# Moving first loads, one broadcast and a load schedule at the opening of a kernel's second pass

## The chip, the cores and the metric

The kernel runs on one core of a Trainium2 chip. The metric is the device time of one execution in microseconds (us); the number compared is the median of several runs. One further execution is recorded by the hardware profiler, and all line numbers and times inside the kernel come from that one.

## What is computed

The layer mixes two branches of the same input `x` (2048 rows of 576), and the kernel returns the output and the gradients of seven tensors (`B_x` is a constant and is not used):

```python
g = sigmoid((x * gate_w).sum(-1))              # one gate per row
a = irfft2(rfft2(x) * (w_r + 1j * w_i))        # branch A: a spectral filter
b = (gelu(x @ w_gate) * (x @ w_up)) @ w_down   # branch B: hidden width 4608
out = g * a + (1 - g) * b
# returned: out, and the gradients of x, w_r, w_i, w_gate, w_up, w_down, gate_w for grad_out
```

## The kernel before

**Two passes.** Pass one goes over the hidden width in 18 groups. It computes the hidden activations and their gradients, writes both to DRAM scratch (`scr`), forms the gradients of the three weight matrices, and beside this work runs the forward transforms of branch A and of its gradient. It leaves the spectra in DRAM scratch (`scr_p1` for the output, `scr_p2` for the gradient of `x`). Pass two, from about 919 us on, goes over the 16 row tiles of 128 rows. It multiplies the scratch by `w_down` (job "b", the output of branch B), by the transposed `w_gate` (job "g") and by the transposed `w_up` (job "u"); "g" and "u" of a tile add into one pair of accumulators and give the gradient of `x`. The last tile has both in one job "x". The list `jobs` fixes the order: g0, g1, b0 to b9, u0, u1, b10, g2, u2, b11 and so on.

**One job.** A job has three slices of 12 x 128 hidden columns. A slice is one tile `pin`, loaded from `scr` by a transposing DMA on SyncE's queue (L1120); it feeds two *blocks* of 12 matmuls (`block`, L1194), one for each half of the 576 output columns. So a job is 6 blocks or 72 matmuls. `ensure` keeps `pin` loads six tiles ahead, as many as there are buffers. At the head of each job from the second on, one of the nine loads that fill `wuT`, the transposed `w_up`, is issued (`load_wuT`, L1153), on the same SyncE queue. `wuT` is first read by u0, the thirteenth job.

**The way back of the transform.** Each row tile of branch A has four *pieces*: two `z_piece` (L1244: six matmuls of a folded spectrum `F` with the table `RT`, then two copies `Z` on ScalarE) and two `d_piece` (L1254: six matmuls of `Z` with the table `It`). `w` = 0 is the output, `w` = 1 the gradient. `F` comes from `fold` (L1221 to L1237): 17 small VectorE instructions on a loaded tile `Vp`. `load_p` (L1210) brings `Vp` from scratch by ScalarE's DMA queue; it has four buffers. The pieces are dropped between blocks by `tick`: a counter goes up by one at every block once the first "b" job has begun, and a piece is emitted when the counter reaches `ticks[1]`; after that the next is due three or four blocks later, provided that fewer than five finished tiles of `w` = 1 wait for use. In the kernel before, the first piece comes after two blocks of b0.

**Tables.** `build_RT` and `build_I` make `RT` and `It` on the core: GpSimd writes index rows, VectorE turns them into angles, ScalarE takes sines (L222, L203).

**The broadcast.** `spread_gw` copies `gate_w` to all 128 partitions: two matmuls by a column of ones (L1185) into a pair of accumulators, and two VectorE copies to `gwf` (L1186). `gwf` is read when a tile's gradient is finished, first after u0.

**Around the border of the passes.** Three SyncE loads bring `w_down` into `wd_all` (L1139) while pass one ends; the last weight gradients are copied from the accumulator `wps` to `dw` on ScalarE (L587) and stored by ScalarE's queue (L643).

**Order.** The schedule is manual: each engine executes its instructions in the order in which the source emits them. All accumulators of pass two are one pool of eight PSUM banks, taken in pairs; a pair is handed out again once its last reader is done. The banks are handed out in the order 0, 7, 6, 5, 4, 3, 2, 1, and bank 7 is that of the last `wps`, the accumulator that pass one closes with. The DMAs issued by SyncE and ScalarE share eight completion semaphores, given out in turn, and a DMA waits until the one eight places before it, on the same semaphore, has landed.

In the kernel before, the order at the opening of pass two is: tables, first four `load_p`, folds of tile 0, then the jobs; `spread_gw` stands at the head of the second job, so on TensorE between g0 and g1, and on VectorE behind the two folds.

Of the kernel before, what the change touches and what calls it, by code (L numbers as in the profile page):

```python
# [12 lines left out]
F32 = mybir.dt.float32  # L13
# [7 lines left out]
P, T = 128, 16  # L21
# [22 lines left out]
def eo(c):  # L44

    return slice(c, 512, 4)
# [16 lines left out]
def iotas(nc, res, unit):  # L63
    tb = Tables()
    G, V = nc.gpsimd, nc.vector
    kw = dict(allow_small_or_imprecise_dtypes=True)
    tb.halfpi = res.tile([P, 1], F32, name="halfpi")
    V.memset(tb.halfpi[:], math.pi / 2)
    tb.pi = res.tile([P, 1], F32, name="pi")
    V.memset(tb.pi[:], math.pi * EPS_SCALE)  # L70
    tb.warm = res.tile([P, 1], F32, name="warm")
    nc.scalar.activation(tb.warm[:], tb.halfpi[:], ACT.Sin)
    tb.lrow = unit([QF], F32, name="lrow")
    G.iota(tb.lrow[:], pattern=[[1, QF]], base=0, channel_multiplier=0, **kw)
    tb.dcol = res.tile([P, 5], F32, name="dcol")
    G.iota(tb.dcol[:, 0:4], pattern=[[1, 4]], base=0, channel_multiplier=4, **kw)
    for r in (LO, HI):
        G.iota(tb.dcol[r, 4:5], pattern=[[0, 1]], base=512, channel_multiplier=1, **kw)
    tb.dn = res.tile([P, 5], F32, name="dn")
    V.tensor_scalar(tb.dn[:], tb.dcol[:], 1.0 / D, None, op0=ALU.mult)  # L80
    tb.late = []
    tb.Dt = []
    tb.Rt = []
    return tb
# [87 lines left out]
def build_I(nc, tb, ftile, small, out):  # L172

    V = nc.vector
    R = slice(0, 2 * LQ)
    col = small([8])
    lp, ge, mul, add, e0, e1, half, q_ = (col[R, k:k + 1] for k in range(8))
    X, y = ftile()[R], ftile()[R]

    def ts(o, i, x, y, op0=ALU.mult, op1=ALU.add):  # L180
        V.tensor_scalar(o, i, x, y, op0=op0, op1=op1)

    def tt(o, a, b, op):
        V.tensor_tensor(o, a, b, op=op)
    kw = dict(allow_small_or_imprecise_dtypes=True)
    nc.gpsimd.iota(q_, pattern=[[0, 1]], base=0, channel_multiplier=1, **kw)
    nc.gpsimd.iota(X.rearrange("p (r q) -> p r q", r=6), pattern=[[1, 6], [6, 96]], base=0, channel_multiplier=0, **kw)
    V.tensor_scalar(ge, q_, float(LQ), None, op0=ALU.is_ge)
    ts(lp, ge, -float(LQ), 0.0)
    tt(lp, lp, q_, ALU.add)  # L190
    ts(mul, ge, -2.0, 1.0)
    tt(mul, mul, lp, ALU.mult)
    ts(add, ge, -float(D // 4), float(D // 4))
    ts(X, X, mul, add)
    ts(y, X, 1.0 / D, MAGIC)
    ts(y, y, -MAGIC, -float(D), op0=ALU.add, op1=ALU.mult)
    tt(X, X, y, ALU.add)
    V.tensor_scalar(e0, lp, 0.0, None, op0=ALU.is_equal)
    V.tensor_scalar(e1, lp, float(LQ - 1), None, op0=ALU.is_equal)
    tt(half, e0, e1, ALU.add)  # L200
    ts(half, half, -0.5, 1.0)
    o = out[R].rearrange("p r q -> p (r q)")
    nc.scalar.activation(o, X, ACT.Sin, scale=2.0 * math.pi / D * EPS_SCALE)  # L203
    V.tensor_scalar(o, o, half, None, op0=ALU.mult)


def build_RT(nc, tb, ftile, out):

    V = nc.vector
    kw = dict(allow_small_or_imprecise_dtypes=True)  # L210
    w = ftile()
    row, base, ts, off = w[:, 0:P], w[:, P:2 * P], w[:, 2 * P:2 * P + T], w[:, 2 * P + T:2 * P + 2 * T]
    nc.gpsimd.iota(row, pattern=[[1, P]], base=0, channel_multiplier=0, **kw)
    nc.gpsimd.iota(ts, pattern=[[1, T]], base=0, channel_multiplier=0, **kw)
    V.tensor_scalar(base, row, tb.kc[:, 0:1], None, op0=ALU.mult)
    V.tensor_scalar(off, ts, tb.kc[:, 1:2], tb.kc[:, 2:3], op0=ALU.mult, op1=ALU.add)
    for t0 in range(0, T, 4):
        X = ftile(I32)[:, 0:4 * P]
        for t in range(4):
            V.tensor_scalar(X[:, t * P:(t + 1) * P], base, off[:, t0 + t:t0 + t + 1], None, op0=ALU.add)  # L220
        V.tensor_single_scalar(X, X, S - 1, op=ALU.bitwise_and)
        nc.scalar.activation(out[:, t0:t0 + 4, :].rearrange("p t m -> p (t m)"), X, ACT.Sin, bias=tb.pi[:],  # L222
                             scale=-2.0 * math.pi / S * EPS_SCALE)
# [101 lines left out]
def kernel(  # L325
# [4 lines left out]
    nc = tc.nc  # L330
# [80 lines left out]
    tb = iotas(nc, res, unit)  # L411
# [458 lines left out]
    for c in range(6):  # L870
        w = gwr[0:1, eo(c)] if c < 4 else gwr[0:1, 512:D]
# [279 lines left out]
    def load_wuT(k, r0):  # L1151
        f0 = k * FCB + r0
        LD.dma_start_transpose(wuT[k][:, r0:r0 + 4, :], B_w_up[:, f0 * P:(f0 + 4) * P])  # L1153
# [3 lines left out]
    with tc.tile_pool(name="p2f", bufs=3, **kw) as p2f, \  # L1157
# [14 lines left out]
        wT_loads = [(k, r0) for k in range(NB) for r0 in (0, 4, 8)]  # L1172
# [10 lines left out]
        def spread_gw():  # L1183
            for h, ps in enumerate(acc_pair()):
                nc.tensor.matmul(ps[:, :288], lhsT=onesr[:], rhs=gwr[:, h * 288:(h + 1) * 288], start=True, stop=True)  # L1185
                V.tensor_copy(gwf[:, h * 288:(h + 1) * 288], ps[:, :288])  # L1186

        def acc_pair():
            return [pacc.tile([P, 512], F32, tag="acc", name="acc") for _ in range(2)]
# [9 lines left out]

        RT = sp.tile([P, T, P], BF16, name="RTt")  # L1200
        It = sp.tile([P, 6, 96], BF16, name="It")
        build_RT(nc, tb, f32t, RT)
        build_I(nc, tb, f32t, lambda shape: p2s.tile([P] + shape, F32, tag="icol", name="icol", bufs=1), It)
        srcs_v = [q[:].rearrange("g (k t c) l -> (g k) t c l", k=4, c=2) for q in (scr_p1, scr_p2)]
        vp, ft, zt = {}, {}, {}
        spec = [{}, {}]
# [1 line left out]
        def load_p(i, w):  # L1208
            vp[i, w] = sp.tile([P, 2, DF], BF16, tag="Vp", name="Vp", bufs=4)
            nc.scalar.dma_start(vp[i, w][:], srcs_v[w][:, i])  # L1210

        def fold(i, w):
            v = vp.pop((i, w))
            up = v[:, :, 96:288].rearrange("p c (j l) -> p c j l", j=2)[:, :, :, 0:LQ]
# [44 lines left out]
        def piece(i, k):  # L1259

            def f():
                (z_piece, d_piece)[k // 2](i, k % 2)
                if k == 0 and i + 2 < T:
                    load_p(i + 2, 0)
                if k == 1:
                    load_xd(i)
                    if i + 2 < T:
                        load_p(i + 2, 1)
                    if i + 1 < T:
                        fold(i + 1, 0)  # L1270
                if k == 2 and i + 1 < T:
                    fold(i + 1, 1)
                if k == 3:
                    posts()
            return f
        pieces = [piece(i, k) for i in range(T) for k in range(4)]
        for i in range(2):
            for w in range(2):
                load_p(i, w)
        for w in range(2):  # L1280
            fold(0, w)
        ticks = [0, 2]

        def tick(on):
            ticks[0] += on
# [4 lines left out]
        def need(i):  # L1290
            while i not in spec[1]:
                pieces.pop(0)()
# [10 lines left out]
        def posts():  # L1303
            while posted[0] in bos and posted[0] in spec[0]:
                post(posted[0])
                posted[0] += 1

        def b_job(t):
            bps = acc_pair()
            bo = bos[t] = p2bo.tile([P, D], BF16, tag="bo", name="bo")  # L1310
            for f0 in range(0, NFC, FCB):
                At = loaded.pop((0, t, f0))
                for h in range(2):
                    block(bps[h], h, At, lambda r: wd_all[:, f0 + r], f0 == 0, f0 + FCB == NFC)
                    tick(1)
                    if f0 + FCB == NFC:
                        nc.scalar.copy(bo[:, h * 288:(h + 1) * 288], bps[h][:, :288])
                used[0] += 1
                ensure()
# [58 lines left out]
        def x_end(t):  # L1378
            pre = x_pre(t)
            o1 = b16t()  # L1380
            for h in range(2):
                x_out(t, h, pre, o1, ST)
            accs.pop(t)
# [10 lines left out]
                x_out(t, h, pre, o1, LD)  # L1394

        for i, (kind, t) in enumerate(jobs):
            if i > 0 and wT_loads:
                load_wuT(*wT_loads.pop(0))
            if i == 1:
                spread_gw()  # L1400
            if kind == "b":
                b_job(t)
                posts()
            elif kind == "g":
                x_half(t, 1)
            elif kind == "u":
                x_half(t, 2)
                need(t)
                assert posted[0] > t
                x_end(t)  # L1410
            else:
                need(t)
                assert posted[0] > t
                gate_grad()
                x_last(t)
# [30 lines left out]
```

## Time and profile before

| what | value |
|---|---|
| median of 3 runs | 1376.17 us (1375.54 to 1377.75) |
| the profiled execution: its own time | 1375.8 us |
| the profiled execution: span from first to last instruction | 1374.0 us |
| TensorE (PE) busy | 1354.6 us, 99% |
| VectorE (DVE) busy | 844.1 us, 61% |
| ScalarE (ACT) busy | 751.6 us, 55% |
| GpSimd (POOL) busy | 259.8 us, 19% |
| mean busy share of the 16 DMA engines in the 40 slices of pass two | mostly 0.9 or more until the last eight slices |

The names: PE is the matmul stream and PEld its weight loads; SPq and ACTq are the queues that issue DMAs from SyncE and ScalarE. L1194 is line 1194 of the kernel before. A matmul's own duration overlaps with its neighbour's, so the distance from start to start is what it costs. A DMA share above 1 says that packets of several queues overlap on an engine. An engine that is idle costs time only where the chain that ends last runs through it.

### The profile page before, as it was taken

The page shows a single profiled execution, that of the slowest core. Times are in us where ns is not written, and L with a number is a line of the kernel's source. Part 1 is how long each engine was busy: PE and PEld are TensorE (multiplying, and loading weights), DVE is VectorE, ACT ScalarE, POOL GpSimd, SP SyncE. Part 2 cuts the span into 40 slices and gives each one's busy share as a digit, 9 for nine tenths or more (in the row PEclk, how much of TensorE's full clock was granted, in tenths as well). Part 3 has the DMA queues.
Part 4 walks back from the last instruction along what each step waited for, and adds up shares of the span by engine and source line. Part 5 has one row for each costly group of instructions (what it writes and reads, how often), then busy time and mean ns, then how long its engine had stood idle before and what let it go on. Part 6 is the DMA issues. An engine that isn't in the chain of part 4 may idle for free.

```text
span 1374.0 us, 26478 instructions
## 1 busy us (share of the span) xinstructions
PE 1354.6 (99%) x10199; PEld 905.7 (66%) x10280; DVE 844.1 (61%) x1976; ACT 751.6 (55%) x1360; POOL 259.8 (19%) x508
## 2 busy tenths in 40 slices
PE   9999999999999999999999999998999999999998
PEld 7566656656655656655655665566888888888886
DVE  7886766776658786786687655625535543545320
ACT  7886767766767776776777676621333322223210
POOL 5210110111314432442441311100000000000000
PEclk9999999999999999999999999999999999999999
DMA  7435435435644754754664657499999888779773
GB/s 231 135 88 142 136 97 146 122 108 150 166 115 121 191 133 129 189 136 134 173 148 127 167 155 170 110 284 191 202 217 182 171 171 157 166 157 172 158 147 73
DMA packets 497397, 211.85 MB, mean 154 GB/s; under 512 B 307219, under 2 KB 488150, under 8 KB 497270
## 3 DMA queue, kind: packets, MB, share of 16 engines
q1 hardware_dynamic: 470932, 175.30, 55.3%
q0 software_dynamic: 14912, 24.24, 6.2%
q10 hardware_dynamic: 11426, 10.61, 3.4%
q8 instruction: 80, 1.31, 0.4%
q14 instruction: 47, 0.39, 0.1%
HBM read 43.13 MB, written 93.56 MB: 99 GB/s over the span
## 4 chain that ended last, share of the span: by engine, by line
PE 94%; DVE 2%; DMA 1%; issue 1%; ACT 1%; SPq 0%; ACTq 0%; POOL 0%; DVEq 0%; POOLq 0%
PE acc L1194 30%; PE xy L506 17%; PE wps L636 17%; PE wps L618 10%; PE z L490 9%; PE wps L650 2%; PE xy L499 2%; PE z L495 2%; DMA wd_all<-in_B_w_down_dram 1%; PE acc L1244 1%; PE pf L679 1%; PE acc L1254 1%; PE pf L697 1%; PE pf L682 1%; PE pf L839 1%
## 5 line engine op out<-in xcount | busy, mean ns | idle before, releaser
L1194 PEld LDWEIGHTS <-pin 128*128 128x128 bf16 x3456 | 336.0, 98 | 84.0 <-issue 0.3
L506 PE MATMUL xy<-wgu,xT 128*128 128x512 bf16 x1086 | 258.7, 379 | 8.5 <-issue 7.5
L636 PE MATMUL wps<-dH,xn 128*128 128x512 bf16 x1137 | 264.9, 379 | 0.9
L636 PEld LDWEIGHTS <-xn 128*128 128x128 bf16 x1152 | 112.5, 98 | 126.5 <-issue 0.6
L506 PEld LDWEIGHTS <-xT 128*128 128x128 bf16 x1152 | 106.8, 98 | 133.1 <-issue 24.8
L643 POOL DMA_DIRECT2D out_dram<-dw x134 | 72.9, 547 | 416.6 <-ACT dw L587 399.1
L618 PE MATMUL wps<-dB,A 128*128 128x288 bf16 x1152 | 149.6, 286 | 0.0
L1194 PE MATMUL acc<-wd_all,pin 128*128 128x288 bf16 x1152 | 148.9, 289 | 0.0
L1194 PE MATMUL acc<-wgT,pin 128*128 128x288 bf16 x1152 | 147.0, 286 | 0.0
L1194 PE MATMUL acc<-wuT,pin 128*128 128x288 bf16 x1152 | 146.0, 286 | 0.0
L1256 ACT ACTIVATE yo<-acc 128x288 bf16<-128x288 f32 x64 | 67.4, 1247 | 129.2 <-PE acc L1254 106.4
L490 PE MATMUL z<-wdT,dOT 128*128 128x256 bf16 x1152 | 137.7, 273 | 0.1
L618 PEld LDWEIGHTS <-A 128*128 128x128 bf16 x1152 | 112.7, 98 | 34.1
L518 ACT ACTIVATE da<-z,omg 128x256 bf16<-128x256 f32 x288 | 112.1, 472 | 34.5 <-PE z L495 34.4
L490 PEld LDWEIGHTS <-dOT 128*128 128x128 bf16 x1152 | 112.4, 98 | 21.7 <-DVE dOT L462 0.3
L1375 DVE TENSOR_TENSOR b16t<-acc,f32t 128x288 bf16<-128x288 f32 x32 | 14.7, 458 | 175.9 <-PE acc L1194 175.9
L527 ACT CAST xb<-xy 128x512 bf16<-128x512 f32 x144 | 85.3, 592 | 48.5 <-PE xy L506 48.5
L525 ACT ACTIVATE q<-xy 128x512 bf16<-128x512 f32 x144 | 88.4, 616 | 4.9 <-PE xy L506 3.4
L564 DVE TENSOR_TENSOR xb<-xb,sg 128x1024 bf16<-128x1024 bf16 x48 | 33.1, 690 | 94.3 <-ACT sg L556 94.3
L1246 ACT CAST Z<-acc 98x384 bf16<-98x384 f32 x64 | 27.5, 481 | 113.5 <-PE acc L1244 113.5
L528 ACT CAST hu<-xy 128x512 bf16<-128x512 f32 x144 | 87.6, 608 | 0.0
L587 ACT CAST dw<-wps 128x512 bf16<-128x512 f32 x72 | 42.3, 589 | 67.0 <-PE wps L636 66.0
(523 smaller groups left out, 1741.2 us busy)
## 6 DMA issues: line engine op xcount, KB each, us to landing
scr<-dH SPq DMA_DIRECT2D x144, 256.0 KB, 3.6
scr<-A SPq DMA_DIRECT2D x72, 256.0 KB, 2.7
out_dram<-dw POOLq DMA_DIRECT2D x134, 64.0 KB, 2.3
wd_all<-in_B_w_down_dram SPq DMA_DIRECT2D x3, 1728.0 KB, 10.4
out_dram<-dwd POOLq DMA_DIRECT2D x34, 144.0 KB, 3.0
scr_p<-Vt SPq DMA_DIRECT2D x32, 144.5 KB, 2.6
Vp<-scr_p ACTq DMA_DIRECT2D x32, 144.5 KB, 4.3
wgu<-in_B_w_gate_dram SPq DMA_DIRECT2D x18, 256.0 KB, 4.3
```

What stands on the lines that cost most here:

```text
L490: nc.tensor.matmul(zo(t), lhsT=dOT[:, ci, t, :], rhs=wdT[:, ci, :], start=(t % 4 < 2 and ci == 0), stop=False)
L506: nc.tensor.matmul(xy[k][:, t % 2, :], lhsT=xT[:, ci, t, :], rhs=wgu[:, ci, :], start=False, stop=(ci == 3))
L518: nc.scalar.activation(da[:, t, :], z[:, t % 2, t // 2, :], ACT.Copy, scale=omg32[:, 4 * m + t:4 * m + t + 1])
L525: nc.scalar.activation(q[:, h, :], xy[:, :, 0:FG], ACT.Square)
L527: nc.scalar.copy(xb[:, h, :], xy[:, :, 0:FG])
L528: nc.scalar.copy(hu[:, h, :], xy[:, :, FG:2 * FG])
L587: wcopy[0](out, in_)
L618: nc.tensor.matmul(wps[:, :288], lhsT=tl(0, t)[:, fch * P:(fch + 1) * P], rhs=dB[:, t, h * 288:(h + 1) * 288], start=(t == 0), stop=(t == ...
L636: nc.tensor.matmul(wps[:].rearrange("p a b -> p (a b)"), lhsT=xn[:, t, c * P:(c + 1) * P], rhs=kt[t // 4][1][:, t % 4].rearrange("p k f -> ...
L643: wst[0].dma_start(ov[:, c, fsl], dw[:, k, :])
L1194: nc.tensor.matmul(acc[:, :288], lhsT=src[:, r, :], rhs=w_of(r)[:, h * 288:(h + 1) * 288], start=(first and r == 0), stop=(last and r == F ...
L1256: nc.scalar.activation(yv[:, 3 * b:3 * b + 3], ps[:, 0:288].rearrange("p (r q) -> p r q", r=3), ACT.Copy, scale=(SD2, 1.0)[w])
```

## The change

Three edits, all at the opening of pass two:

- the first four `load_p` and `spread_gw` are emitted ahead of `build_RT` and `build_I` (before, the loads came after the tables and the broadcast at the head of the second job);
- the first piece is due at tick 4 in place of tick 2;
- the `w_up` loads begin at the head of the fourth job (b1) in place of the second (g1), still one a job.

```diff
         RT = sp.tile([P, T, P], BF16, name="RTt")
         It = sp.tile([P, 6, 96], BF16, name="It")
-        build_RT(nc, tb, f32t, RT)
-        build_I(nc, tb, f32t, lambda shape: p2s.tile([P] + shape, F32, tag="icol", name="icol", bufs=1), It)
...
         def load_p(i, w):
             vp[i, w] = sp.tile([P, 2, DF], BF16, tag="Vp", name="Vp", bufs=4)
             nc.scalar.dma_start(vp[i, w][:], srcs_v[w][:, i])
-
+        for i in range(2):
+            for w in range(2):
+                load_p(i, w)
+        spread_gw()
+        build_RT(nc, tb, f32t, RT)
+        build_I(nc, tb, f32t, lambda shape: p2s.tile([P] + shape, F32, tag="icol", name="icol", bufs=1), It)
...
         pieces = [piece(i, k) for i in range(T) for k in range(4)]
-        for i in range(2):
-            for w in range(2):
-                load_p(i, w)
         for w in range(2):
             fold(0, w)
-        ticks = [0, 2]
+        ticks = [0, 4]
...
         for i, (kind, t) in enumerate(jobs):
-            if i > 0 and wT_loads:
+            if i > 2 and wT_loads:
                 load_wuT(*wT_loads.pop(0))
-            if i == 1:
-                spread_gw()
             if kind == "b":
                 b_job(t)
                 posts()
```

## The prediction

> **What bounds the kernel now.** I read the page first, then the list of waits, then the instructions of each engine in order of time around the one place that stood out.
>
> ```profile
> span 1374.0 us, 26478 instructions
> PE 1354.6 (99%) x10199; PEld 905.7 (66%) x10280; DVE 844.1 (61%) x1976; ACT 751.6 (55%) x1360; POOL 259.8 (19%) x508
> PE   9999999999999999999999999998999999999998
> ```
>
> TensorE is busy in every slice but one, the 28th (slices are 34.35 us, so 927 to 962 us). A change that adds no matmul and removes none can gain only what TensorE waits there, and lose only by new waits. The waits of TensorE, all of them (total us, times, longest):
>
> ```profile
> PE xy L506 <- issue: 7.5, 47, 0.2
> PE acc L1244 <- DVE gwf L1186: 4.6, 1, 4.6
> PE pf L868 <- POOL ident masks.py:199: 1.4, 1, 1.4
> PE pf L445 <- DVE dOT L452: 0.2, 1, 0.2
> ```
>
> One wait of 4.6 us, at the first way-back piece, ended by the copy of the broadcast. TensorE around it, then the same stretch as sums (columns: stretch, PE, PEld, DVE, ACT, POOL busy, granted clock, DMA share, GB/s):
>
> ```profile
> 937.38 3.10 PE L1194 MATMUL acc<-wd_all,pin 128*128 128x288 bf16 x24
> 945.06 0.88 PE L1244 MATMUL acc<-RTt,F 128*98 128x128 bf16 x6 [4.58 <-DVE gwf L1186]
> 945.73 8.45 PE L1194 MATMUL acc<-wd_all,pin 128*128 128x288 bf16 x48
> 954.02 0.50 PE L1244 MATMUL acc<-RTt,F 128*98 128x128 bf16 x6
> 943.80:950.60 6.80, 5.54 (x27) 3.78 (x28) 6.77 (x37) 0.86 (x2) 0.00 (x0) 0.50 1.27 199
> 950.60:954.20 3.60, 3.60 (x33) 2.93 (x32) 0.78 (x4) 0.40 (x1) 0.00 (x0) 0.99 0.75 147
> ```
>
> The idle time is only part of the loss. After it, 48 matmuls take 8.24 us on the chain of work that ended last (945.94 to 954.18), where 48 elsewhere take 5.88; the clock stands at 0.50 from 943.8 to 950.6.
>
> **What holds the copy back.** VectorE and ScalarE ahead of it:
>
> ```profile
> 919.49 0.58 ACT L587 CAST dw<-wps 128x512 bf16<-128x512 f32 x1 [2.87 <-PE wps L636]
> 922.67 1.09 ACTq L643 DMA_DIRECT2D out_dram<-dw  x2
> 925.08 1.33 ACT L222 ACTIVATE RTt<-f32t,pi 128x512 bf16<-128x512 int32 x2
> 932.26 1.96 ACTq L1210 DMA_DIRECT2D Vp<-scr_p  x4
> 938.41 0.36 DVE L1221 TENSOR_TENSOR pm<-Vp 128x196 f32<-128x196 bf16 x1 [5.08 <-DMA Vp<-scr_p]
> 941.15 0.36 DVE L1237 SCALAR_TENSOR_TENSOR F<-wp__11709 128x196 bf16<-128x196 f32 x1
> 944.55 0.82 DVE L1186 COPY gwf<-acc 128x288 f32<-128x288 f32 x2
> ```
>
> ScalarE issues the `Vp` loads only after the last sine; VectorE waits 5.08 us for the first, folds twice (3.0 us each), and only then copies the broadcast out of the accumulators that the piece wants.
>
> **Part 1, the wait that goes.** With the broadcast first, its accumulators are read by about 921 us and no longer hold the piece. The saving: idle 4.58; the six piece matmuls 0.88 in place of 0.34 on the chain, 0.54; the 48 behind them 8.24 - 5.88 = 2.36. Sum 7.48 us. Check: from 937.38 to 954.18 is 16.80 us, for 72 matmuls at 5.88/48 = 0.1225 (8.82), a piece (0.34) and a first matmul's latency (0.16): 9.32; the difference is 7.48.
>
> **Part 2, the broadcast's new place on TensorE.** Before, it stood between g0 and g1 and cost 928.55 - 928.20 = 0.35 us. Now it is the first thing after pass one. Its first matmul goes to bank 0 at 919.29, as g0 did. Its second goes to bank 7, that of pass one's last `wps`, which ScalarE empties from 919.49 to 920.07; before, g0 came to that bank only with its second block, 1.47 us later. So the second matmul starts at about 920.13, g0 at 920.25 in place of 919.29: +0.96, less the 0.35 that leaves the later place, +0.61 us. Bounds: 0 if the bank is not waited for; for the clock, gaps of 0.2 us cost none and the 4.58 us gap cost 2.9, so up to 0.61 + 2.9. I take 0.61, as 0.7 us of idle is nearer to 0.2.
>
> **Part 3, loads ahead of the tables, on ScalarE's queue.** The loads now stand behind the two `dw` stores (issued until 923.76) and ahead of the sines. The third finds the semaphore of the last `wd_all` load, issued at 917.24 and landed at 927.67. That such a wait holds ScalarE is in the trace: the first `dw` store of 922.67 had its data at 920.07 and went out when a `wd_all` load landed at 922.59. So the third and fourth leave at about 927.7 to 928.5, the table load for sines (1.28 us) follows, and the sines start at 929.9 instead of 925.08, +4.8. The chain through sines and angles ended at 933.3; it ends at 938.1. By then `Vp` has been there for some 7 us, so the fold starts at 938.1 (before: 938.4) and `F` is ready at 941.2. The loads' gain is thus eaten by the tables' delay; alone it would move nothing. VectorE's own two copies (0.82 us, near 920) lie under this wait of the sines. Bounds: if the third load isn't held, `F` is ready near 938.5; if `wd_all` lands 1 to 3 us later because two `Vp` loads share the DMA engines (share 1.15 to 1.26 there), near 942 to 944.
>
> **Part 4, the first piece at tick 4.** Piece one now stands behind four blocks of b0: 937.38 + 0.61 + 4 x 1.47 = 943.87. `F` at 941.2 has 2.7 us in hand; at tick 2 (940.93) it would have been waited for. Costs: none. I walked the counter through the job list: each piece to the third of tile 8 comes exactly two blocks later, then the limit of five finished tiles holds both orders and they are equal. No piece is forced at a "u" job's end.
>
> **Part 5, `w_up` loads two jobs later.** Nine loads, now in b1 to b9, all in jobs at full speed; before, the first two fell into g1 and b0, beside the wait. The price is on SyncE's queue:
>
> ```profile
> 955.66 4.30 SPq L1153 DMA_TRANSPOSE wuT<-in_B_w_up_dram  x1
> 1016.06 2.82 SPq L1153 DMA_TRANSPOSE wuT<-in_B_w_up_dram  x1
> ```
>
> These are the third and the ninth load: six jobs' worth of loads in 60.40 us, 10.07 a job. TensorE's jobs in that stretch take 9.33 (7 blocks with two pieces every 10.89 us, by 6/7). So the queue falls behind by 0.73 us a job. Following each `pin` tile from landing to its first weight load (24 to a tile), the lead is 9.5 to 11 us after the wait and 2.75 at the worst, the tile of 1020.51, landed 1029.07, used 1031.81. In the changed kernel b1 starts with about the same full lead, since no `w_up` load stands before it; the third load's place is the same; then two more jobs slip. The tiles of those jobs had 5.7 and 8.1 us in hand; one load is about 3.4 us of queue, so one and two loads leave 2.3 and 1.3 (more if the slip flattens: the last three intervals average 9.6). The last load itself: the ninth went out 6 us after the job at whose head it stands had begun (1010.05), so in the changed kernel it goes out 6 to 8 us into b9, 1 to 3 us before u0, and lands 5.1 to 10.4 us later (median 7.1): about 4 to 6 us into u0, whose last third begins to read it at 6.2 and its own four columns at 7.2. I take nothing for both, but this is the thinnest cover of the change: bounds 0 and, from the longest landings (8.6 and 10.4), some 3 us.
>
> **Sum.** -7.48 + 0.61 = -6.87 us. Profiled execution: 1375.8 to 1368.9; against the median of the runs, 0.37 us higher, 1369.3.
>
> **A rule on the clock.** The row: 3.3 us after TensorE went idle the clock fell, and it stayed at 0.50 for 5.5 us after work resumed. [...] I keep the row: it is this stall.
>
> **Rivals.**
> - *A small wait remains* (0.28): `F` comes after 943.87, a `pin` tile in b8 to u0 lands late, or the last `w_up` load does. For: the slip of 0.73 us a job, leads of 1 to 2 us. Against: no `pin` or `wuT` wait in the trace before. Up to 3.3 us of idle, the length that the clock outlasted: 1369.3 to 1372.6, likely near 1370.8.
> - *The wait only changes its releaser* (0.09): the last `wd_all` load lands 6 us later, or the copies still come late. `F` at 947.2, idle 3.3 plus 2.9 of slow clock: 6.2 of the 6.87 are gone, 1375.5. The same holds if the change does not free the accumulators.
> - *Starved at the end of the `w_up` loads* (0.05, slower): if the queue slips by 2 us a job instead of 0.73, the lead is used up in five jobs, and the remaining four owe 8 us, which come as gaps; two long enough to drop the clock add 5.8. 13.8 - 6.9 = +6.9: 1383. It turns slower than before from a slip of 1.9 us on (9 x 1.9 - 10 = 7), from less where gaps drop the clock. Against: the measured slip.
>
> **How the numbers follow.** The forecast, 0.58: 1369.3, its own range 1367.7 (no bank wait, 1368.3 from the profiled time, less the 0.63 between the lowest run and the median) to 1370.0. The range goes on to the first rival's end, 1372.6. 0.2% is 2.75 us, about what a measurement of this kernel can tell from no change: faster is below 1373.4. Forecast and first rival lie there, 0.86; the second within, 0.09; slower 0.05.
>
> **What would show it.** Right: no TensorE wait on `gwf`, the clock at full speed through 930 to 960; a wait of some 0.7 us at L1185's second matmul; the sines 4 to 5 us later behind the third `Vp` load; piece one near 944; `pin` leads of 1 to 3 us around b8 and b9. Wrong: a wait of L1244 on `F`, or of L1194 on `pin` or `wuT`, in the list of waits.

## The result and the profile after

The changed kernel takes 1369.53 us (median of 4 runs, 1369.38 to 1369.64) against 1376.13 us before (4 runs, 1375.54 to 1377.75): ratio 0.9949, 95% interval 0.9935 to 0.9964. Its profiled execution took 1369.38 us. From its page:

```profile
span 1367.6 us, 26560 instructions
PE 1361.4 (100%) x10280; PEld 904.5 (66%) x10280; DVE 843.7 (62%) x1976; ACT 751.4 (55%) x1360; POOL 260.8 (19%) x508
PE   9999999999999999999999999999999999999998
```

The 8 in the 28th slice is gone. The waits of TensorE, all of them:

```profile
PE pf L868 <- POOL ident masks.py:199: 1.4, 1, 1.4
PE acc L1185 <- ACT dw L587: 0.4, 1, 0.4
PE pf L461 <- ACT Dt L155: 0.3, 1, 0.3
PE pf L445 <- DVE dOT L452: 0.2, 1, 0.2
```

The wait of 4.6 us on `gwf` is gone; the 0.4 us at L1185 is the new one that part 2 of the prediction named. The row of 7.5 us at L506 in the list before is not part of the gain: it lies in pass one and goes with matmul records that the profile before lacks (10199 of 10280). A second profile of the changed kernel, with 10199 records too, has the same row and a span of 1367.4 us. The stretch that ran at half clock before, as sums (same columns as there):

```profile
943.80:950.60 6.80, 6.80 (x62) 5.54 (x61) 6.80 (x42) 1.66 (x4) 0.00 (x0) 1.00 0.77 157
```

TensorE is busy throughout and the clock stands at 1.00. The opening in order of time (L1208 is `load_p` here, L1240 the last line of `fold`, L1247 the first matmul of a piece):

```profile
919.84 0.29 PE L1185 MATMUL acc<-gwr,onesr 1*128 1x288 bf16 x1
919.94 0.59 ACT L587 CAST dw<-wps 128x512 bf16<-128x512 f32 x1 [2.87 <-PE wps L636]
920.58 0.28 PE L1185 MATMUL acc<-gwr,onesr 1*128 1x288 bf16 x1 [0.45 <-ACT dw L587]
924.18 6.44 ACTq L1208 DMA_DIRECT2D Vp<-scr_p  x4
930.65 1.28 ACT L222 ACT_TABLE_LOAD   x1 [10.12 <-DMA Vp<-scr_p]
931.94 1.33 ACT L222 ACTIVATE RTt<-f32t,pi 128x512 bf16<-128x512 int32 x2
942.83 0.36 DVE L1240 SCALAR_TENSOR_TENSOR F<-wp__11715 128x196 bf16<-128x196 f32 x1
944.32 0.50 PE L1247 MATMUL acc<-RTt,F 128*98 128x128 bf16 x6
```

The second L1185 matmul waits for the last copy of pass one. The four `Vp` issues take 6.44 us, because the third is held until 928.37, when the last `wd_all` load has landed (928.35), and the sines come after them. `F` is there at 943.19, the piece at 944.32.

**Where the time went.** I cut each profile at four events of TensorE: the start of pass one's last `wps` matmul, and the first weight load of b0, b1 and u0.

| profile | last wps to b0 | b0 to b1 | b1 to u0 | u0 to the end |
|---|---|---|---|---|
| before | 18.19 | 17.04 | 83.73 | 335.99 |
| changed | 18.79 | 9.15 | 84.20 | 335.93 |
| difference | +0.60 | -7.89 | +0.47 | -0.06 |

The +0.47 belongs to the -7.89: with tick 4 one piece moves from the b0 stretch to the next. Sum -6.88; pass one was 0.46 us longer in this profile, so the span differs by 6.4.

### The profile page after: what moved, and what is told of

Read it like the earlier page. It is cut to its first block, busy times and chain, and to the rows that moved or that the text cites. A ratio compares the mean times of both kernels' runs of the same rounds, so it can differ in the third digit from the quotient of the medians.

```text
span 1367.6 us, 26560 instructions
## 1 busy us (share of the span) xinstructions
PE 1361.4 (100%) x10280; PEld 904.5 (66%) x10280; DVE 843.7 (62%) x1976; ACT 751.4 (55%) x1360; POOL 260.8 (19%) x508
## 4 chain that ended last, share of the span: by engine, by line
PE 98%; DVE 1%; ACT 1%; issue 0%; POOL 0%; POOLq 0%; DVEq 0%
PE acc L1194 31%; PE xy L506 18%; PE wps L636 18%; PE wps L618 10%; PE z L490 9%; PE wps L650 2%; PE xy L499 2%; PE z L495 2%; PE acc L1247 1%; PE pf L679 1%; PE acc L1257 1%; PE pf L697 1%; PE pf L682 1%; PE pf L839 1%; PE pf L761 1%; PE pf L445 0%
## 5 line engine op out<-in xcount | busy, mean ns | idle before, releaser
L506 PE MATMUL xy<-wgu,xT 128*128 128x512 bf16 x1152 | 270.6, 380 | 0.0
L506 PEld LDWEIGHTS <-xT 128*128 128x128 bf16 x1152 | 106.7, 98 | 133.2 <-issue 24.8
L1259 ACT ACTIVATE yo<-acc 128x288 bf16<-128x288 f32 x64 | 67.5, 1247 | 133.6 <-PE acc L1257 110.8
```

The costliest lines, as they stand in the source:

```text
L506: nc.tensor.matmul(xy[k][:, t % 2, :], lhsT=xT[:, ci, t, :], rhs=wgu[:, ci, :], start=False, stop=(ci == 3))
L1259: nc.scalar.activation(yv[:, 3 * b:3 * b + 3], ps[:, 0:288].rearrange("p (r q) -> p r q", r=3), ACT.Copy, scale=(SD2, 1.0)[w])
```

## The experiments

**Theory T** is the prediction's: the gain is one wait of TensorE, for accumulators that the broadcast's copies held, and the slow clock behind it. **R1**: the earlier `Vp` loads bring it. **R2**: the `w_up` loads bring it by leaving the DMA engines. The kernels ran in three groups of four, each group on another chip; each group shares its runs of the kernel before, so a ratio is against the kernel before of the same group. First the medians, then the stretches of the profile of each. The profile is one execution and need not be the median one: with the broadcast alone it is the slowest of twelve runs, with tick 4 alone the second slowest.

| kernel | us, median (range) | ratio to before (interval) | wps to b0 | b0 to b1 | b1 to u0 |
|---|---|---|---|---|---|
| before, group 1 | 1378.09 (1372.90 to 1384.02) | | | | |
| broadcast alone | 1376.01 (1372.87 to 1381.07) | 0.9988 (0.9973 to 1.0004) | 18.79 | 13.75 | 91.54 |
| loads alone | 1374.36 (1369.96 to 1377.55) | 0.9970 (0.9955 to 0.9985) | 18.19 | 11.02 | 90.18 |
| tick 4 alone | 1377.97 (1373.36 to 1381.05) | 0.9997 (0.9981 to 1.0014) | 18.19 | 11.49 | 93.88 |
| w_up alone | 1377.70 (1372.39 to 1385.82) | 1.0000 (0.9980 to 1.0020) | 18.19 | 15.54 | 83.73 |
| before, group 2 | 1376.55 (1372.04 to 1384.06) | | | | |
| changed | 1369.58 (1369.03 to 1371.51) | 0.9943 (0.9923 to 0.9962) | 18.79 | 9.15 | 84.20 |
| changed, w_up as before | 1370.19 (1369.62 to 1375.64) | 0.9949 (0.9931 to 0.9967) | 18.79 | 9.16 | 85.02 |
| changed, tick 2 | 1376.85 (1368.95 to 1377.58) | 0.9985 (0.9964 to 1.0005) | 18.79 | 9.56 | 91.65 |
| changed, loads as before | 1369.34 (1368.88 to 1369.81) | 0.9944 (0.9927 to 0.9962) | 18.79 | 9.15 | 84.20 |
| before, group 3 | 1378.33 (1371.06 to 1385.44) | | | | |
| broadcast and tick 4 | 1375.36 (1369.06 to 1379.46) | 0.9964 (0.9945 to 0.9982) | 18.79 | 9.15 | 90.52 |
| changed, tick 2, GpSimd loads | 1376.18 (1373.91 to 1379.19) | 0.9983 (0.9970 to 0.9996) | 18.79 | 9.56 | 90.14 |
| broadcast in g1, folds behind it | 1368.91 (1368.62 to 1369.10) | 0.9924 (0.9904 to 0.9944) | 18.19 | 9.15 | 84.19 |
| the same, GpSimd loads | 1371.75 (1369.15 to 1378.32) | 0.9954 (0.9932 to 0.9976) | 18.19 | 9.15 | 89.06 |

The stretch from u0 to the end is 335.5 to 336.0 us in all of them. The b1 to u0 stretch at full speed is 83.73 with tick 2 and 84.20 with tick 4. The kernel before is not steady: 1371 to 1385 over 91 runs, where its profile above happens to have no wait in b1 to b9. No second execution of it was profiled.

### The broadcast alone

```diff
         RT = sp.tile([P, T, P], BF16, name="RTt")
         It = sp.tile([P, 6, 96], BF16, name="It")
+        spread_gw()
...
-            if i == 1:
-                spread_gw()
```

> The kernel before with one edit: the broadcast alone moved ahead of the tables; loads, first piece (tick 2) and w_up loads as before. Theory T (the gain is TensorE's wait for accumulators that the broadcast's copies hold, with the slow clock behind it): piece one is due near 941.1 us of the span, F is ready near 941.5 because Vp still lands near 938.3, so a wait of about 0.5 us on F remains, no slow clock; 1376.1 - 7.5 + 0.6 + 0.5 = 1369.7 us. Rival R1 (the gain comes from the earlier Vp loads): no gain, about 1376. Rival R2 (it comes from the w_up loads that leave the DMA engines): no gain, about 1376.

Measured 1376.01. TensorE's waits in its profile (L1245 and L1255 are the first matmuls of a `z_piece` and a `d_piece`):

```profile
PE acc L1194 <- DMA pin<-scr: 3.9, 2, 3.5
PE acc L1245 <- DVE F L1236: 1.7, 1, 1.7
PE acc L1255 <- ACT bo L1318: 1.6, 1, 1.6
PE acc L1245 <- DVE F L1237: 0.5, 1, 0.5
```

The wait on `gwf` is gone, as T says, and others stand in its place: on `F`, on `pin` in b7 and b9, and on an accumulator of a "b" job that ScalarE had not emptied. T's time was wrong twice. At the opening it had 0.5 us of waiting for `F` and no slow clock; there were 1.66 and 0.53 us, and then a granted clock of 0.50 from 943.56 to 946.97. And it did not look beyond the opening.

### The loads alone

```diff
         It = sp.tile([P, 6, 96], BF16, name="It")
-        build_RT(nc, tb, f32t, RT)
-        build_I(nc, tb, f32t, ...)
...
+        for i in range(2):
+            for w in range(2):
+                load_p(i, w)
+        build_RT(nc, tb, f32t, RT)
+        build_I(nc, tb, f32t, ...)
...
         pieces = [piece(i, k) for i in range(T) for k in range(4)]
-        for i in range(2):
-            for w in range(2):
-                load_p(i, w)
```

> The kernel before with one edit: the first four Vp loads alone ahead of the tables. T: the copies of the broadcast still stand behind both folds, and the tables end some 6 us later (ScalarE is held by the third and fourth load), so the folds end near 946 and the copy near 947: TensorE waits some 6 us in place of 4.6 and the clock falls as before; 1377 to 1379 us, slower than before by about 2. R1: Vp is there early, faster by 4 to 7, 1369 to 1372. R2: 1376.

Measured 1374.36: neither. The opening of its profile:

```profile
924.16 1.93 ACTq L1208 DMA_DIRECT2D Vp<-scr_p  x4
927.41 1.33 ACT L222 ACTIVATE RTt<-f32t,pi 128x512 bf16<-128x512 int32 x2
941.72 0.82 DVE L1186 COPY gwf<-acc 128x288 f32<-128x288 f32 x2
942.23 0.69 PE L1247 MATMUL acc<-RTt,F 128*98 128x128 bf16 x6 [1.10 <-DVE gwf L1186]
```

The four issues take 1.93 us, not 6.44: in this order of the program the third load does not share the semaphore of the last `wd_all` load (which lands at 928.30 here), but that of a `dw` store landed at 920.05; all four are out by 926.09. So the sines begin 4.5 us earlier than in the changed kernel, and the broadcast is waited for 1.10 us only. The early loads do gain at the opening when nothing holds them. In this profile the gain is lost again in b1 to b9 (90.18 in place of 83.73); over the twelve runs a gain of 0.3% is left.

### Tick 4 alone

```diff
-        ticks = [0, 2]
+        ticks = [0, 4]
```

> The kernel before with one edit: the first piece at tick 4 in place of 2. T: piece one is due near 943.4, the first copy of the broadcast ends at 945.0; TensorE waits about 1.6 us in place of 4.6. [...] If a wait of 1.6 us drops the clock as well, 1373. R1 and R2: as before, 1376.

Measured 1377.97, where I expected 1370.2 if the clock held (1376.1 - 7.5 + 1.6). At the opening T came close: a wait of 1.98 us for the 1.6, a granted clock of 1.00 from 941.89 to 948.71, and 11.49 in place of 17.04 from b0 to b1. But b1 to u0 gave all of it back: two waits of 1.5 and 4.5 us on accumulators that ScalarE emptied late. The stretch is 9.68 us longer than in the changed kernel, more than the 5.9 us of these waits, and the granted clock of the whole profiled execution is 0.997 on average, against 1.000 there. In front of the late copies ScalarE stood 4.9 us for a `pin` load and 7.8 us for a `w_up` load; the kernel with tick 2, below, shows how.

### The w_up loads alone

```diff
-            if i > 0 and wT_loads:
+            if i > 2 and wT_loads:
```

> The kernel before with one edit: the w_up loads two jobs later. T: VectorE waits for Vp, which lands at 938.3 with a w_up load beside it; without that load it may land up to 1 us earlier, and the wait of TensorE shrinks by as much: 1375 to 1376.2 us. R2: most of the gain is here, 1369 to 1371. R1: 1376. In the trace I look at the lead of the pin tiles in b6 to b9 too: by the prediction's slip of 0.73 us a job it falls to 1 to 3 us.

Measured 1377.70, ratio 1.0000; so R2 falls as the whole cause. The wait is 4.11 us in place of 4.58. The loads left every 10.0 us, and the lead of `pin` fell to 1.2 us without a wait.

### The changed kernel again

No edit.

> The changed kernel itself, beside the next three. In the four runs with one edit the w_up loads left SyncE's queue every 10.0 to 10.9 us a job, in the first profile of the changed kernel every 9.45, and TensorE's job takes 9.33. Theory T2 (two gains: the broadcast frees the first piece, and the w_up loads' later start keeps the pin tiles' lead whole until it is needed): nine jobs at 10.0 to 10.4 use up 6 to 10 us of a lead of 10.5, no or little starvation: 1369 to 1372. Rival R3 (the w_up loads' place is worth nothing, the chip alone was slower in those runs): 1373 to 1377 here, with waits on pin in b8 to u0.

1369.58, while the kernel before ran from 1372 to 1384 beside it. So the changed kernel has gained steadiness as well as time: its nine runs lie within 2.5 us, the 29 of the kernel before within 12. The `w_up` loads left every 9.86 us, and the lead fell to 3.8 us.

### The changed kernel with one edit undone

The `w_up` loads back at the second job:

```diff
-            if i > 2 and wT_loads:
+            if i > 0 and wT_loads:
```

> The changed kernel with the w_up loads back at the head of the second job. T2: as in the run with the broadcast alone, loads in g1 and b0 meet w_down, dw, Vp and pin on the DMA engines, the lead is down to 5 to 7 us when b2 begins and is gone by b7 or b8: a wait on pin of 2 to 4 us with a drop of the clock, 1373 to 1377. T (the prediction: the place of the w_up loads costs or gains nothing, or its late place costs): 1369 to 1370, equal to the changed kernel or better.

1370.19, one run of eleven at 1375.6. The time is near T's, with T2's signs in part: the lead did fall to 5 us by b2 and to 3 later, but was not used up; a wait of 0.7 us on ScalarE is left. The loads' place is worth 0.6 us between the medians here.

Tick 2:

```diff
-        ticks = [0, 4]
+        ticks = [0, 2]
```

> The changed kernel with the first piece at tick 2 again. The piece is then due near 941.4 us and F is ready near 943.2 (both from the profile of the changed kernel): TensorE waits about 1.8 us. [...]

1376.85, twelve runs from 1368.95 to 1377.58, seven of them from 1376.7 up. I expected a wait on `F`, so 1371.3 us, or 1373 to 1374 if the clock fell, and there is no such wait: `F` was ready at 941.53, just when the piece was due (its sines began 1.7 us earlier than in the changed kernel's first profile). The loss is far from the opening, in b8 (L1301 loads `x_t` and `do_t`; L1317 copies a "b" job's result; L1257 and L1259 are a `d_piece`):

```profile
1012.79 4.17 SPq L1153 DMA_TRANSPOSE wuT<-in_B_w_up_dram  x1
1016.13 0.34 ACTq L1301 DMA_DIRECT2D do_t<-in_grad_out_dram  x1
1023.27 0.33 ACTq L1208 DMA_DIRECT2D Vp<-scr_p  x1
1023.64 0.40 ACT L1317 CAST bo<-acc 128x288 bf16<-128x288 f32 x1 [9.32 <-DMA wuT<-in_B_w_up_dram]
1024.09 0.40 PE L1257 MATMUL acc<-It,Z 98*128 98x96 bf16 x3 [6.01 <-ACT bo L1317]
```

Read upward: TensorE waits 6.01 us for an accumulator, because ScalarE's copy `bo` comes late; ScalarE stood 9.32 us in front of it. Up to 1016.13 it was held at the issue of `do_t`, behind a `pin` load; from there to 1023.2 at the issue of a `Vp` load whose semaphore is that of the `w_up` load of 1012.79, slow to land (10.4 us). In `b_job` the counter is stepped ahead of the copy of the same block; so where a piece with loads falls on a job's last block, its DMA issues stand ahead of the copy on ScalarE. The second piece of a tile issues three loads; with tick 2 it falls on the ends of b0 and b7, with tick 4 on the end of b5. (The first piece of a tile issues one `Vp` load; it falls on the end of b4 with tick 2, of b2 and b9 with tick 4.)

The loads behind the tables:

```diff
-        for i in range(2):
-            for w in range(2):
-                load_p(i, w)
         spread_gw()
         build_RT(nc, tb, f32t, RT)
         build_I(nc, tb, f32t, ...)
+        for i in range(2):
+            for w in range(2):
+                load_p(i, w)
```

> The changed kernel with the first four Vp loads back behind the tables; broadcast, tick 4 and w_up as changed. Prediction's part 3 (the early loads alone move nothing: what Vp gains the tables lose): Vp lands near 938.3, F is ready near 941.5 to 943, piece one is due at 944.3: no wait, equal to the changed kernel within 1 us. Rival R1 (the early loads carry the gain): 1373 or more.

1369.34, as expected, with `F` ready earlier than expected. The early loads carry nothing in the changed kernel:

```profile
937.24 0.36 DVE L1240 SCALAR_TENSOR_TENSOR F<-wp__11715 128x196 bf16<-128x196 f32 x1
944.02 0.50 PE L1247 MATMUL acc<-RTt,F 128*98 128x128 bf16 x6
```

`F` is ready 6.4 us ahead of the piece without them, and 1.1 us with them.

### Broadcast and tick 4 without the rest

The kernel before with two edits:

```diff
+        spread_gw()
         build_RT(nc, tb, f32t, RT)
...
-        ticks = [0, 2]
+        ticks = [0, 4]
...
-            if i == 1:
-                spread_gw()
```

> The kernel before with two edits: the broadcast ahead of the tables and the first piece at tick 4; loads behind the tables and w_up loads from the second job on, as before. T3 (two separate things: the opening wait, removed by broadcast plus tick 4; and waits in b3 to b9, which come when SyncE's queue is late and ScalarE is held at a DMA issue until a slow w_up load, which shares its semaphore, has landed): no wait at the opening; in b3 to b9 leads of 1 to 5 us and now and then a wait, as the w_up loads begin early: 1369.5 to 1373, with some runs higher. T (the opening is all): 1369.5 in every run.

1375.36: five runs of twelve from 1369.1 to 1371.2, seven from 1375.2 to 1379.5. The opening is at full speed (9.15); the profile is of one of the seven (1375.49). Its chain of work that ended last, in b5 to b6:

```profile
994.58 6.86 DMA wuT<-in_B_w_up_dram
1001.47 0.02 ACTq L1211
1001.52 0.33 ACTq L1211
1001.90 0.41 ACT bo L1318
1002.35 0.40 PE acc L1255 x3
```

The same hold, in the place where tick 4 has it: a slow `w_up` load, the `Vp` issue behind it, the copy, the piece. The changed kernel has that place too, and there the `Vp` load waits for the same `w_up` load, the one issued at the head of b5. From its first profile:

```profile
986.86 3.58 SPq L1153 DMA_TRANSPOSE wuT<-in_B_w_up_dram  x1
995.67 0.40 ACTq L1208 DMA_DIRECT2D Vp<-scr_p  x1
996.11 0.40 ACT L1317 CAST bo<-acc 128x288 bf16<-128x288 f32 x1 [0.75 <-issue]
```

Here the `w_up` load landed at 993.67, 2 us before the `Vp` issue. What differs is how late SyncE's queue sends that load after b5 has begun:

| profile | `w_up` sent after b5 began, us | TensorE waits for the late copy, us |
|---|---|---|
| changed (two profiles) | 2.1 and 1.9 | 0 |
| broadcast in g1, folds behind it | 5.4 | 0 |
| changed, loads as before | 5.6 | 0 |
| changed, w_up as before | 6.9 | 0.7 |
| tick 4 alone | 9.6 | 4.5 |
| broadcast and tick 4 | 10.0 | 3.4 |

So the hold on ScalarE comes when SyncE's queue has fallen behind, and that is also what eats the lead of `pin`. With tick 2 (1376.85) the load in question, at the head of b7, went out 9.0 us after b7 had begun. The table also shows what the loads and the `w_up` edit do: either of them alone, added to broadcast and tick 4, left the queue less far behind at b5 (6.9 and 5.6 in place of 10.0), both together least. These are single profiles.

### ScalarE relieved of its loads

Tick 2, with `Vp`, `x_t` and `do_t` issued by GpSimd:

```diff
-            nc.scalar.dma_start(vp[i, w][:], srcs_v[w][:, i])
+            nc.gpsimd.dma_start(vp[i, w][:], srcs_v[w][:, i])
...
-                nc.scalar.dma_start(tl[:], v[:, t, :])
+                nc.gpsimd.dma_start(tl[:], v[:, t, :])
```

> The changed kernel with tick 2, which gave 1376.85 with a wait of 6.0 us in b6 on an accumulator that ScalarE emptied late; here the Vp, x_t and do_t loads are issued by GpSimd's queue instead of ScalarE's, so that no DMA wait can hold ScalarE. T3: that wait is gone; a small wait on pin or F may stay: 1369.5 to 1371.5. Rival R4 (a piece next to a job's end waits for accumulators anyway): the wait stays, 1375 to 1377.

1376.18: T3's time is wrong, and R4's came true for another reason. The wait that R4 foretells is gone with the hold (that wait stood in b8, not in b6), but the time is not better:

```profile
PE acc L1194 <- DMA pin<-scr: 4.4, 4, 2.2
PE acc L1194 <- ACT bo L1317: 0.9, 2, 0.5
```

The waits have moved to `pin`: SyncE's loads left every 11.0 us a job, and the lead was gone by b6.

### A version without the bank wait

Loads behind the tables, the broadcast between g0 and g1 again, the folds of tile 0 behind it:

```diff
         for i, (kind, t) in enumerate(jobs):
...
+            if i == 1:
+                spread_gw()
+                for w in range(2):
+                    fold(0, w)
```

> The changed kernel with loads behind the tables, the broadcast at the head of the second job as before, but the two folds of tile 0 emitted behind it, so that its copies go ahead of them; tick 4 and w_up as changed. The broadcast's second matmul then does not wait for the bank that pass one's last copy empties: 0.6 us less than the changed kernel, 1368.7 to 1369.0, if the prediction's part 2 is right; 1369.5 if it is not.

1368.91 (1368.62 to 1369.10), the lowest median of all and the 0.6 us that part 2 foretells; the changed kernel did not run in this group, so the 0.6 us rest on the stretch from `wps` to b0 (18.19 against 18.79). TensorE's waits are down to two, both in the first 34 us of pass one:

```profile
PE pf L868 <- POOL ident masks.py:199: 1.4, 1, 1.4
PE pf L445 <- DVE dOT L452: 0.2, 1, 0.2
```

Its lead of `pin` fell to 1.4 us and was enough. With GpSimd's loads in the same kernel:

```diff
-            nc.scalar.dma_start(vp[i, w][:], srcs_v[w][:, i])
+            nc.gpsimd.dma_start(vp[i, w][:], srcs_v[w][:, i])
...
-                nc.scalar.dma_start(tl[:], v[:, t, :])
+                nc.gpsimd.dma_start(tl[:], v[:, t, :])
```

> The one before, with the Vp, x_t and do_t loads issued by GpSimd's queue: ScalarE is never held. T3: 1368.7 to 1369.0, and the highest runs come down. If GpSimd's slower issue delays Vp, the first piece waits: 1370 or more.

1371.75, with runs up to 1378.3: `pin` waits of up to 2.9 us, as in the other GpSimd kernel. The first piece did not wait (9.15 from b0 to b1), so the expected slower time came from another place than expected.

## Why the prediction was right, point by point

The forecast was 1369.3 us, the measurement 1369.53.

- **Part 1, the wait that goes: right.** b0 to b1 was 17.04 before; the same two pieces at full speed take 9.56 (the changed kernel with tick 2). 17.04 - 9.56 = 7.48, the number forecast.
- **Part 2, the bank: right.** +0.60 measured, +0.61 forecast; the granted clock is 1.00 from 919 to 945 us. The wait itself is 0.45 us, forecast some 0.7. Undone in the version without the bank wait, it gave the 0.6 us back (18.19).
- **Part 3, the loads: right in kind, too small.** The third load left at 928.37, when the last `wd_all` load had landed (928.35). The fourth issue took 1.88 us, so the sines came 6.4 us late instead of 4.8 (6.86 less the 0.46 by which pass one was longer), and the piece had 1.1 us in hand, not 2.7. "Alone it would move nothing" holds in the changed kernel, where the loads as before gave the same time, and was wrong for the kernel before: there the loads are not held, and the opening in the profile got 6.0 us shorter.
- **Part 4, tick 4: the cost right, the reason wrong.** I wrote that at tick 2 `F` "would have been waited for". In the profiled execution it was not; yet tick 2 costs 7 us in seven of twelve runs, in the profiled one by ScalarE held at a job's end. I had counted when the pieces come, and not what stands behind them on ScalarE's queue.
- **Part 5, the w_up loads: the term was mis-sized.** I took the slip of 0.73 us a job from one profile as a property of the load. In the two profiles of the changed kernel it was 0.12 and 0.53 and the least lead from b1 on 7.5 and 3.8 us; in the version without the bank wait it was 0.84 and the lead 1.4, near the 1.3 forecast. No wait came of it. That the late place *protects* the lead I had not priced: as b2 begins it is 9 to 12 us in the profiles of the changed kernel and of the version without the bank wait, and 5 to 8 in the experiments with the early place (9.5 in the one profile that I had). Nor had I seen that the same lateness of SyncE's queue decides about the hold at the end of b5.
- **What the whole argument missed.** It rested on one execution of the kernel before, without a wait in b1 to b9. The experiments show a second loss there: the single edits gained up to 6 us at the opening in their profiles, and broadcast, loads and tick 4 each lost 6.5 to 9.7 us in b1 to u0. The forecast came out because the changed kernel has neither loss. The runs show why in part (the table of b5 above), but the prediction gave no reason for it, and so far it was luck. It also called 0.2% about what a measurement can tell, with three runs in hand that agreed within 2.2 us; the 91 runs scatter over 14.

**Open.** Why SyncE's loads take 9.5 us a job in one execution and 10 to 11 in another of almost the same program, I did not settle; nor why tick 2 is slow in most runs and the changed kernel in none of those measured. The DMA engines are busiest just there: 0.9 or more of the time in the five slices from 893 to 1065 us of the kernel before (the 40 slices of its page are those of the whole kernel, not of pass two, as the table ahead of the prediction has it). No run undid the broadcast alone. With the loads alone the wait for it was down to 1.10 us, and tick 4 puts the piece later by more than that, so loads and tick 4 with the broadcast left in its old place might have gained as much; this was not tested. That ScalarE's hold is the loss with tick 2 is shown for the profiled execution; removing the hold brought another wait, so its price alone is not measured.

## What to carry to other kernels

Before costing a wait that goes, look at what an engine's queue holds behind each DMA issue: in the changed kernel with tick 2, issues that waited, the longest for a semaphore shared with a `w_up` load that took 10.4 us to land, kept ScalarE's copy back for 9.32 us, and TensorE 6.01 us for the accumulators. A gain at one place can be lost at another: up to 6 us won at the opening went again in b1 to u0, which grew by 6.5 to 9.7. So follow each tile from landing to use, in more than one execution. And profile the kernel before more than once if its runs scatter.

## What the runs showed of the hardware

The clock fell after less idle time than the prediction took as safe (3.3 us). In the kernel with the broadcast alone, two gaps of 1.66 and 0.53 us near 942 were enough (the last line has the columns as before, with the clock and the DMA share near the end):

```profile
942.87 0.26 PE L1245 MATMUL acc<-RTt,F 128*98 128x128 bf16 x1 [1.66 <-DVE F L1236]
943.66 0.77 PE L1245 MATMUL acc<-RTt,F 128*98 128x128 bf16 x5 [0.53 <-DVE F L1237]
943.56:946.97 3.41, 3.31 (x17) 2.29 (x18) 3.41 (x20) 0.86 (x2) 0.00 (x0) 0.50 0.96 178
```

What the other profiles have of gaps and the clock:

| profile | idle before, us | the granted clock, or the pace of the matmuls |
|---|---|---|
| tick 4 alone | 1.98 (to 946.08) | 1.00 from 941.89 to 948.71 |
| changed without the bank wait, GpSimd loads | 2.86 (1033.2 to 1036.1) | 1.00 in the gap, 1.000 on average over the execution |
| broadcast and tick 4 | 3.44 (to 1002.35) | the next 7 matmuls of a job in 1.88 us; 23 in 2.98 before (from 984.84) |
| broadcast alone | 3.5, for `pin` | 0.50 from 1032.31 to 1035.72 |
| before | 4.58 (to 945.06) | 0.50 from 943.8 to 950.6 |
| changed, tick 2 | 6.01 (to 1024.09) | the next 8 matmuls of a job in 2.12 us; 9 in 1.27 before (from 1005.73) |

The length of a single gap does not sort these cases: 1.66 and 0.53 us dropped the clock, 1.98 and 2.86 us did not. What decides was not shown.
